# Reordering the start and the end of a fused retention and MoE kernel: two up projections ahead of their down projections, a shorter load ring, the tail block second to last

## The chip, the cores and the metric

One core of one Trainium2 chip. The metric is the device time of one execution in microseconds. A profiled execution shows a span, from the first to the last instruction, that is about 1.8 us shorter than the time. Engines are named as in the profile: PE (TensorE), PEld (its weight loads), DVE (VectorE), ACT (ScalarE), POOL (GpSimd), SP (the engine that issues most DMAs). In the tables by stage, (x245) counts instructions, and the clock is the mean clock that TensorE was granted, 1.00 being full speed.

## The reference, cut to what matters

```python
# attention with a decay mask and no softmax: q, k, v are (8, 8, 576, 64) float32
scores = scale * (q @ k.T)
ret    = scores * where(i >= j, gamma_h ** (i - j), 0)      # per head h
x      = (ret @ v) -> (4608, 512)
# then an MLP: w_in (512, 2048), w_out (2048, 512)
g      = gelu_tanh(x @ w_in)          # "up"
out    = g @ w_out                    # "down", float32, 4608 rows
```

## The kernel before

A batch has 576 rows: 512 in a block of its own, and 64 that all eight batches put into one ninth "tail" block. Each block has an up projection (64 matmuls of 512 columns, gelu on ScalarE) and a down projection in seven products (`my mz mw mv mu my2 mz2`), a fast-multiplication scheme over quadrants. A product collects in a bank of PSUM, the accumulator memory; the instructions that add it into the output tile `ost`, and so free the bank, are its *settle*. In the lists below `my2` and `mz2` appear as `my` and `mz`, whose banks they use. For it VectorE mixes the gelu output (three `tensor_tensor` per pair of slices: sum `gdia`, sum `gsum`, difference in place) and mixes the second weights once at the start:

```python
    def mix_w_out(j, e):                      # e = (V, A, V, G) before
        r0, r1 = w_raw.pop(("o", 2 * j)), w_raw.pop(("o", 2 * j + 1))
        e[0].tensor_tensor(out=w[:, 0:2, :]..., in0=r1, in1=r0, op=ALU.subtract)
        copy(e[1], w[:, 4, :], r0[:, L]); copy(e[1], w[:, 3, :], r1[:, R])
        e[2].tensor_tensor(out=w[:, 2, :], in0=r0[:, L], in1=r1[:, R], op=ALU.add)
        e[3].tensor_tensor(out=w[:, 5, :], in0=r0[:, L], in1=r0[:, R], op=ALU.add)
        e[3].tensor_tensor(out=w[:, 6, :], in0=r1[:, L], in1=r1[:, R], op=ALU.add)
        done(); done()                        # the two load tiles may be reused
```

Inputs come through a ring of `LD = 20` load tiles of 256 KB, in the order batch 0, all of `w_in`, half of batch 1, all of `w_out`, the rest. In the traces an engine's instructions start in program order (in the changed kernel the settle of `my2` starts at 83.66 us, behind four mixes, though its product ended at 79.0), so the plan, "after unit i of TensorE's work do these steps", is the schedule. The start of it, cut:

```python
    def stream(j):                            # five down products, slice by slice, as w_out arrives
        for m in MS[:5]:
            F.product(m, [j])
    units = A1[0:2] + [f for i in range(2, 8) for f in (A0[i], A1[i])]   # block 0 up
    units += [L(stream, j) for j in range(NJ)]                           # block 0 down
    ...
    units = [L(P.down, "my2"), L(P.down, "mz2")] + A0 + A1 + [L(F2.down, m) for m in MS]  # block 1
    ...
    for t in range(2, B + 1):                 # blocks 2..7, then the tail block (None)
        F = Block(t if t < B else None)
        ...
        run([L(F.up, f) for f in range(NF)] + [L(F.down, m) for m in MS], plan)
        P = F
    P.store()                                 # the tail block: eight DMAs, one per batch
```

Of the kernel before, what the change touches and what calls it, by code (L numbers as in the profile page):

```python
# [19 lines left out]
def kernel(  # L20
# [124 lines left out]
    LD = 20  # L145
# [48 lines left out]

    def tiles(b):
        a = att[b]
        a["kq"] = sb.tile([128, NS, 2, 2, 512], F16, tag="kq", name="kq", bufs=2)
        a["v"] = sb.tile([128, NS, 2, 512], F16, tag="cv", name="cv", bufs=2)
        a["kqt"] = sb.tile([128, 2, 256], F16, tag="kqt", name="kqt", bufs=2)
        a["vt"] = sb.tile([128, 256], F16, tag="cvt", name="cvt", bufs=3)  # L200
        a["T"] = sb.tile([128, NS, 2, 2, 4, 128], F16, tag="T", name="T", bufs=2)
        a["Tt"] = sb.tile([128, 2, 2, 128], F16, tag="Tt", name="Tt", bufs=3)
# [62 lines left out]
    def mix_w_out(j, e):  # L265
        r0, r1 = w_raw.pop(("o", 2 * j)), w_raw.pop(("o", 2 * j + 1))
        L, R = slice(0, 256), slice(256, 512)
        w = w_out_sb[:, j]
        e[0].tensor_tensor(out=w[:, 0:2, :].rearrange("p m c -> p (m c)"), in0=r1, in1=r0, op=ALU.subtract)  # L269
        copy(e[1], w[:, 4, :], r0[:, L])  # L270
        copy(e[1], w[:, 3, :], r1[:, R])
        e[2].tensor_tensor(out=w[:, 2, :], in0=r0[:, L], in1=r1[:, R], op=ALU.add)  # L272
        e[3].tensor_tensor(out=w[:, 5, :], in0=r0[:, L], in1=r0[:, R], op=ALU.add)
        e[3].tensor_tensor(out=w[:, 6, :], in0=r1[:, L], in1=r1[:, R], op=ALU.add)
        done()
        done()
# [49 lines left out]
    def mask_sc(b, s, hh):  # L326
        a = att[b]
        st = a.pop(("st", s, hh))
        for hl in range(2):
            x = sb.tile([128, 512], F16, tag="ret", name="ret", bufs=8)  # L330
            nc.vector.tensor_tensor(  # L331
                out=x.rearrange("p (a m) -> p a m", a=2),
                in0=st[hl].rearrange("p (a m) -> p a m", a=2),
                in1=cm.rearrange("p r s i -> p (r s i)").unsqueeze(1).to_broadcast([128, 2, 256]),
                op=ALU.mult,
            )
            a["ret", s, hh, hl] = x
# [20 lines left out]
    def mask_tail(b):  # L358
        a = att[b]
        st = a.pop("stt")  # L360
        for hl in range(2):
            x = sb.tile([128, 128], F16, tag="rett", name="rett", bufs=4)
# [27 lines left out]
    def scan(b, n):  # L390
# [4 lines left out]
        if n > 0:  # L395
            t = sb.tile([128, HP, 64], F32, tag="vs", name="vs", bufs=2)
            nc.vector.tensor_tensor(out=t, in0=uc, in1=a["w", n - 1], op=ALU.add)  # L397
            uc = t
        w = sb.tile([128, HP, 64], F32, tag="ws", name="ws", bufs=3)
# [90 lines left out]
    class Block:  # L490
        def __init__(self, b):
            self.b = b
            self.gT = self.sc = self.ost = None
            self.bank = {}

        def open(self):
            if self.gT is None:
                self.gT = sb.tile([128, NJ, 2, 512], F16, tag="gT", name="gT", bufs=1)

        def up(self, f):  # L500
# [11 lines left out]
            nc.scalar.activation(out=self.gT[:, f // 2, f % 2], in_=hp, func=AF.Gelu_apprx_tanh)  # L512

        def up_half(self, j, u):
            self.open()
            hp = bank("hp")
            for h in range(2):
# [8 lines left out]
                out=self.gT[:, j].rearrange("p h (s u c) -> p h s u c", s=2, u=2)[:, :, :, u, :],  # L526
# [4 lines left out]
        def mix(self, j, n):  # L531
            if self.sc is None:
                self.sc = sb.tile([128, NJ, 512], F16, tag="gsum", name="gsum", bufs=1)
                self.sa = sb.tile([128, NJ, 256], F16, tag="gdia", name="gdia", bufs=1)
            g = self.gT[:, j : j + n]
            L, R = slice(0, 256), slice(256, 512)
            nc.vector.tensor_tensor(  # L537
                out=self.sa[:, j : j + n], in0=g[:, :, 0, L], in1=g[:, :, 1, R], op=ALU.add
            )
            nc.vector.tensor_tensor(out=self.sc[:, j : j + n], in0=g[:, :, 0], in1=g[:, :, 1], op=ALU.add)  # L540
            nc.vector.tensor_tensor(  # L541
                out=g.rearrange("p j h c -> p j (h c)")[:, :, 256:768].rearrange("p j (h c) -> p j h c", h=2),
                in0=g[:, :, :, L],
                in1=g[:, :, :, R],
# [3 lines left out]
        def product(self, m, js=range(NJ)):  # L548
            lhs, w, more = {
                "my": (lambda j, c: self.gT[:, j, 0, c], 1, False),  # L550
                "mz": (lambda j, c: self.gT[:, j, 1, 256:512][:, c], 0, False),
# [3 lines left out]
                "my2": (lambda j, c: self.gT[:, j, 0, 256:512][:, c], 5, True),  # L555
                "mz2": (lambda j, c: self.gT[:, j, 1, c], 6, True),
# [4 lines left out]
            for u in range(2):  # L561
# [11 lines left out]
        def settle(self, m):  # L573
            if self.ost is None:
                self.ost = sb.tile([128, 2, 2, 512], F32, tag="ost", name="ost", bufs=1)
# [23 lines left out]
        def store(self):  # L599
# [8 lines left out]
            else:  # L608
                for u in range(2):
# [3 lines left out]
                    )  # L613

# [76 lines left out]
    for g in range(4):  # L691
        load_w_in(g)
    load_sc(1, 0)
    for f in range(NF):
        load_w_out(f)
    load_sc(1, 1)
    load_tail(0)
    load_tail(1)
    load(2)
    load(3)  # L700
# [6 lines left out]
    mask()  # L707
    cast_v(0, 0, 0, G)
# [30 lines left out]
    cast_w_in(0, (G, V, A, V))  # L739
    values(0, 1)  # L740
    inter_mm(0, 1, 0)
    evac(0, 1, 0)
    A0[0]()
    inter_mm(0, 1, 1)
    evac(0, 1, 1)
    A0[1]()
    cast_w_in(1, (V, G))
    scan_put(0, 3)

    def stream(j):  # L750
        for m in MS[:5]:
            F.product(m, [j])

    units = A1[0:2] + [f for i in range(2, 8) for f in (A0[i], A1[i])]
    units += [L(stream, j) for j in range(NJ)]
    plan = add({},
        (0, L(cast_w_in, 2, (V, G))),
        (2, L(F.mix, 0, 2)),
        (3, L(tbd_zero, 1, G)),
        (4, L(cast_w_in, 3, (V, G))),  # L760
        (6, L(F.mix, 2, 2)),
        (7, L(tiles, 1), L(cast_some, 1, 0, 0, (V, A, G))),
        (8, L(cast_some, 1, 0, 1, (V, A, G))),
        (9, L(tr, 1, 0, 0, (V, A))),
        (10, L(tr, 1, 0, 1, (V, A)), L(F.mix, 4, 2)),
        (11, L(score, 1, 0, 0), L(score, 1, 0, 1)),
        (13, L(state_mm, 1, [0]), L(scan_put, 1, 0), L(scan_put, 1, 1)),
        (14, L(F.mix, 6, 2)),
        *[(12 + j // 2, L(mix_w_out, j, (V, A, V, G))) for j in range(NJ)],
        (16, L(new_x, 1), L(values, 1, 0), L(inter, 1, 0)),  # L770
    )
    run(units, plan)
    for m in MS[:5]:
        F.settle(m)
# [4 lines left out]
    P = F  # L779
    units = [L(P.down, "my2"), L(P.down, "mz2")] + A0 + A1 + [L(F2.down, m) for m in MS]  # L780
    plan = add({},
        (0, L(cast_some, 1, 1, 0, (V, A, G))),
        (1, L(cast_some, 1, 1, 1, (V, A, G)), L(tr, 1, 1, 0, (V, A))),
        (2, L(tr, 1, 1, 1, (V, A)), L(P.store)),
        (3, L(score, 1, 1, 0), L(score, 1, 1, 1), L(state_mm, 1, [1])),
        (4, L(cast_tail, 0, V, V), L(scan_put, 1, 2), L(scan_put, 1, 3)),
        (5, L(tr_tail, 0, V)),
        (6, L(values, 1, 1), L(score_tail_mm, 0), L(inter, 1, 1), L(mask_tail, 0)),
        (8, L(cast_tail, 1, V, V)),
        (9, L(tr_tail, 1, V), L(values_tail, 0), L(inter_tail, 0)),  # L790
        (10, L(score_tail_mm, 1), L(mask_tail, 1)),
        (11, L(values_tail, 1), L(inter_tail, 1)),
        (11, L(tiles, 2), L(cast_some, 2, 0, 0, (V, V, G))),
        (12, L(F2.mix, 0, 2), L(cast_some, 2, 0, 1, (V, V, G))),
        (13, L(tr, 2, 0, 0, (V, A)), L(cast_some, 2, 1, 0, (V, V, G))),
        (14, L(F2.mix, 2, 2), L(tr, 2, 0, 1, (V, A)), L(cast_some, 2, 1, 1, (V, V, G))),
        (15, L(score, 2, 0, 0), L(score, 2, 0, 1)),
        (16, L(F2.mix, 4, 2), L(tr, 2, 1, 0, (A, A))),
        *states(2, 15),
        (18, L(F2.mix, 6, 2), L(tr, 2, 1, 1, (A, A))),  # L800
        (19, L(second, 2), L(cast_tail, 2, V, V)),
        (20, L(tr_tail, 2, A)),
        *casts(3, [17, 18, 19, 20, 21]),
        (22, L(tr_dma, 3), L(load, 4)),
        (22, L(third, 2)),
# [3 lines left out]
    for t in range(2, B + 1):  # L809
        F = Block(t if t < B else None)  # L810
        b = t + 1
# [4 lines left out]
        nxt = t + 2 if t + 2 < B else None  # L816
        if t == 2:
            add(plan,
                (1, L(values_tail, 2), L(inter_tail, 2)),
                *states(3, 3),  # L820
                (5, L(first, 2, False)),
                (9, L(second, 3)),
                (13, L(third, 3)),
                *states(nxt, 15),
            )
        else:
            if t < B:
                add(plan, (1, L(first, t)))
            if b < B:
                add(plan, (6, L(second, b)), (11, L(third, b)))  # L830
            if nxt is not None:
                add(plan, *states(nxt, 15))
        if t + 2 < B:
            add(plan, *casts(t + 2, [0, 2, 4, 6, 8]), (9, L(tr_dma, t + 2)))
            if t + 3 < B:
                add(plan, (9, L(load, t + 3)))
        run([L(F.up, f) for f in range(NF)] + [L(F.down, m) for m in MS], plan)
        P = F
    P.store()
# [30 lines left out]
```

## Time and profile before

| | before |
|---|---|
| time, median | 329.43 us when the prediction was made (3 runs), 328.93 with a fourth |
| span of the profiled execution | 324.0 us (that execution took 325.83, the fast end of its spread) |
| first up matmul to block 2's first up | 18.76 to 111.66 us, TensorE idle 17.8 of 92.9 |
| block 2's first up to the last product | 111.66 to 317, TensorE idle 1.13 of 205.34 |
| last VectorE instruction to the end | 6.4 us |

The stage table, the waits and the end are shown in the prediction. These are three lines of TensorE in order of time; the bracket gives the idle time just before the instruction and what ended it.

```profile
44.21 0.61 PE L563 MATMUL my<-w_out_sb,gT 128*128 128x256 f16 x2 [2.95 <-DVE w_out_sb L269]
48.99 0.38 PE L563 MATMUL my<-w_out_sb,gT 128*128 128x256 f16 x2 [1.10 <-DVE w_out_sb L269]
54.22 0.38 PE L563 MATMUL my<-w_out_sb,gT 128*128 128x256 f16 x2 [1.25 <-DVE w_out_sb L269]
```

Each is the first product of a new slice j. At full clock TensorE consumes a slice in about 1.1 us (one starts at 55.58, the next at 56.67) and before each of these three it had to wait for VectorE to mix it.

### The profile page before, as it was taken

Reading aid. Unit: us, or ns where it says so; the run is one execution under the profiler, and the core shown is the slowest. Engines: PE = TensorE matmul, PEld = TensorE weight load, DVE = VectorE, ACT = ScalarE, POOL = GpSimd, SP = SyncE. Lnnn points to the kernel's source line nnn. Section 1 sums busy time; section 2 is a strip of 40 time slices with the busy share of each in tenths; the row PEclk is TensorE's granted clock in tenths of the full one; section 3 lists DMA queues with packets and bytes.
Section 4 is the critical chain, followed back from the end, with each engine's and each line's share of the span. In section 5 each row is a group of like instructions: output and inputs, shape, how many; then the busy total and the mean of one; then the engine's idle time right before and its main releaser. Section 6 shows DMA issues by size and latency. Waiting matters only on the chain.

```text
span 324.0 us, 8575 instructions
## 1 busy us (share of the span) xinstructions
PE 292.0 (90%) x3628; PEld 206.3 (64%) x3628; DVE 230.9 (71%) x423; ACT 150.5 (46%) x286; POOL 94.5 (29%) x129
## 2 busy tenths in 40 slices
PE   6769857989396998999999999999999999999991
PEld 4648635778285754785587568557855874784680
DVE  5866999877997679958866997697479254443440
ACT  6556635356255066435552545354455316406510
POOL 2536994141941631830165047100000000000000
PEclk9578979999789999999999999999999999999997
DMA  7999983989979898809994996570030011003004
GB/s 216 317 380 297 390 221 88 256 253 276 229 147 250 201 252 235 216 16 242 216 231 131 188 287 143 164 116 2 2 131 0 2 67 65 0 2 129 3 0 130
DMA packets 94438, 52.59 MB, mean 162 GB/s; under 512 B 38848, under 2 KB 88000, under 8 KB 94400
## 3 DMA queue, kind: packets, MB, share of 16 engines
q1 hardware_dynamic: 94208, 51.53, 61.1%
q8 instruction: 28, 0.46, 0.6%
q10 hardware_dynamic: 192, 0.52, 0.6%
q14 instruction: 10, 0.08, 0.1%
HBM read 36.70 MB, written 9.44 MB: 142 GB/s over the span
## 4 chain that ended last, share of the span: by engine, by line
PE 64%; DVE 2%; ACT 0%; issue 0%
PE hp L508 29%; PE my L563 8%; PE mz L563 8%; PE mv L563 4%; PE mu L563 4%; PE mw L563 4%; PE xs L421 2%; PE xs L452 2%; PE st L318 1%; DVE ret L331 1%; PE us L383 1%; PE xs L477 0%; PE xs L434 0%; DVE ws L400 0%; ACT tbd L211 0%; DVE vs L397 0%
## 5 line engine op out<-in xcount | busy, mean ns | idle before, releaser
L512 ACT ACTIVATE gT<-hp 128x512 f16<-128x512 f32 x112 | 66.7, 597 | 77.8 <-PE hp L508 77.5
L508 PE MATMUL hp<-x,w_in_sb 128*128 128x512 f16 x384 | 87.0, 379 | 0.0
L508 PEld LDWEIGHTS <-w_in_sb 128*128 128x128 f16 x448 | 42.8, 98 | 47.4 <-issue 0.3
L563 PEld LDWEIGHTS <-gT 128*128 128x128 f16 x576 | 56.1, 98 | 13.5 <-DVE w_out_sb L269 3.1
L218 POOL TENSOR_TENSOR cv<-ld,sc 128x512 f16<-128x512 f32 x32 | 35.9, 1127 | 43.2 <-DMA ld<-in_v_dram 35.5
L211 POOL CAST kq<-ld 128x512 f16<-128x512 f32 x40 | 27.9, 718 | 54.0 <-PE hp L508 18.3
L331 DVE TENSOR_TENSOR ret<-st,cm 128x512 f16<-128x512 f32 x64 | 40.6, 693 | 1.9 <-PE st L318 1.9
L563 PE MATMUL my<-w_out_sb,gT 128*128 128x256 f16 x288 | 36.0, 275 | 5.4 <-DVE w_out_sb L269 5.3
L563 PE MATMUL mz<-w_out_sb,gT 128*128 128x256 f16 x288 | 35.9, 274 | 0.0
L519 PE MATMUL hp<-x,w_in_sb 128*128 128x256 f16 x256 | 34.7, 292 | 1.1 <-ACT w_in_sb L211 1.1
L211 ACT CAST tbd<-ws 64x256 f16<-64x256 f32 x64 | 25.8, 403 | 19.5 <-DVE ws L400 18.7
L537 DVE TENSOR_TENSOR gdia<-gT 128x512 f16<-128x512 f16 x36 | 17.4, 484 | 23.7 <-ACT gT L512 21.0
L563 PEld LDWEIGHTS <-gsum 128*128 128x128 f16 x288 | 28.4, 99 | 3.4
L580 DVE TENSOR_TENSOR ost<-ost,mv 128x512 f32<-128x512 f32 x18 | 11.6, 684 | 25.4 <-PE mv L563 20.4
L519 PEld LDWEIGHTS <-w_in_sb 128*128 128x128 f16 x256 | 25.8, 105 | 5.8 <-ACT w_in_sb L211 1.3
L540 DVE TENSOR_TENSOR gsum<-gT 128x1024 f16<-128x1024 f16 x36 | 28.0, 779 | 0.0
L541 DVE TENSOR_TENSOR gT<-gT 128x1024 f16<-128x1024 f16 x36 | 27.0, 749 | 1.2
L525 ACT ACTIVATE gT<-hp 128x512 f16<-128x512 f32 x32 | 19.0, 598 | 18.6 <-PE hp L519 18.4
L465 DVE TENSOR_TENSOR x<-xs,gx 128x512 f16<-128x512 f32 x32 | 20.7, 683 | 3.5 <-PE xs L452 3.1
L563 PE MATMUL mw<-w_out_sb,gdia 128*128 128x256 f16 x144 | 18.6, 274 | 1.0 <-DVE w_out_sb L272 0.6
L563 PE MATMUL mv<-w_out_sb,gsum 128*128 128x256 f16 x144 | 18.6, 275 | 0.0
L563 PE MATMUL mu<-w_out_sb,gsum 128*128 128x256 f16 x144 | 18.6, 275 | 0.0
(75 smaller groups left out, 304.7 us busy)
## 6 DMA issues: line engine op xcount, KB each, us to landing
ld<-in_k_dram SPq DMA_DIRECT2D x32, 256.0 KB, 5.5
ld<-in_q_dram SPq DMA_DIRECT2D x32, 256.0 KB, 5.6
ld<-in_v_dram SPq DMA_DIRECT2D x32, 256.0 KB, 5.7
out_dram<-ost SPq DMA_DIRECT2D x16, 512.0 KB, 3.8
ld<-in_moe_w_in_dram SPq DMA_DIRECT2D x16, 256.0 KB, 6.0
ld<-in_moe_w_out_dram SPq DMA_DIRECT2D x16, 256.0 KB, 5.4
ld<-in_k_dram SPq DMA_DIRECT2D x16, 64.0 KB, 4.3
ld<-in_q_dram SPq DMA_DIRECT2D x16, 64.0 KB, 3.4
```

The costliest lines, as they stand in the source:

```text
L211: (eng.copy if eng is nc.scalar else eng.tensor_copy)(out=out, in_=in_)
L218: eng.tensor_tensor(out=unperm(att[b]["v"][:, s, hh, :]), in0=perm(att[b].pop(("v", s, hh))), in1=sc[:, 8 * hh : 8 * hh + 8] .rearrange("p ...
L331: nc.vector.tensor_tensor(out=x.rearrange("p (a m) -> p a m", a=2), in0=st[hl].rearrange("p (a m) -> p a m", a=2), in1=cm.rearrange("p r s ...
L465: nc.vector.tensor_tensor(out=xb[b][:, :, 2 * s + c].rearrange("p s q i -> p q s i"), in0=att[b]["x", s][c].rearrange("p (q s i) -> p q s ...
L508: nc.tensor.matmul(hp, w_in_sb[:, ct, 128 * f : 128 * f + 128], x[:, :, ct, :], start=(ct == 0), stop=(ct == 3),)
L512: nc.scalar.activation(out=self.gT[:, f // 2, f % 2], in_=hp, func=AF.Gelu_apprx_tanh)
L519: nc.tensor.matmul(hp[:, 256 * h : 256 * h + 256], w_in_sb[:, ct, 256 * j + 128 * h : 256 * j + 128 * h + 128], xb[self.b][:, :, 2 * u : 2 ...
L525: nc.scalar.activation(out=self.gT[:, j].rearrange("p h (s u c) -> p h s u c", s=2, u=2)[:, :, :, u, :], in_=hp.rearrange("p (h s c) -> p ...
L537: nc.vector.tensor_tensor(out=self.sa[:, j : j + n], in0=g[:, :, 0, L], in1=g[:, :, 1, R], op=ALU.add)
L540: nc.vector.tensor_tensor(out=self.sc[:, j : j + n], in0=g[:, :, 0], in1=g[:, :, 1], op=ALU.add)
L541: nc.vector.tensor_tensor(out=g.rearrange("p j h c -> p j (h c)")[:, :, 256:768].rearrange("p j (h c) -> p j h c", h=2), in0=g[:, :, :, L] ...
L563: nc.tensor.matmul(t[:, 256 * u : 256 * u + 256], lhs(j, slice(128 * u, 128 * u + 128)), w_out_sb[:, j, w], start=(u == 0 and j == 0 and n ...
```

## The change

Its intent: give TensorE up projections, which need only `w_in` and attention outputs, while `w_out` arrives and is mixed; take casts off VectorE; shorten what follows the last product. The first weights' casts are spread over more engines too. The diff, cut to its core:

```diff
-    LD = 20
+    LD = 12
-        a["T"] = sb.tile([128, NS, 2, 2, 4, 128], F16, tag="T", name="T", bufs=2)
+        a["T"] = big("T").rearrange(...)          # 4 buffers, two of them lent to block 1's gelu output
     # fewer buffers elsewhere: Tt 3 to 2, ret 8 to 6, rett 4 to 2, vs 2 to 1, ws 3 to 2
-            self.gT ... bufs=1      # one tile of 8 slices
+            self.gT ... bufs=2      # two tiles of 4 slices; block 1 takes its two from "T"
-                self.ost = ... bufs=1
+                self.ost = ... bufs=2
     # mix_w_out is split: the last two adds (GpSimd) become mix_w_out2, one unit later
     # loads
-    for g in range(4): load_w_in(g)
-    load_sc(1, 0)
-    for f in range(NF): load_w_out(f)
-    load_sc(1, 1)
+    for g in range(3): load_w_in(g)
+    load_sc(1, 0)
+    load_w_in(3)
+    load_sc(1, 1)
+    for f in range(NF): load_w_out(f)
     # the start
-    units = ...block 0 up, then stream(j) of block 0's down, then block 1 up, then block 1 down
+    units = A1[0:2] + [L(F.up, f) for f in range(4, NF)]                # block 0 up
+    units = A0 + A1                                                     # block 1 up, w_out mixed beside it
+    units = [L(P.down, m) for m in MS] + [L(Q.down, m) for m in MS]     # both downs, batch 2 beside them
+        (0, L(tiles, 2), L(cast_some, 2, 0, 0, (A, A, G))),             # was (V, V, G)
+        (2, L(Q.mix_sa, 0, 4), L(Q.mix_sa, 4, 4)),
+        (4, *[L(Q.mix_sc, 2 * i, 2) for i in range(4)]),
+        (8, *[L(Q.mix_d, 2 * i, 2) for i in range(4)]),
     # the end
-    for t in range(2, B + 1):
+    order = [*range(2, B - 1), None, B - 1]                             # tail block second to last
+        F.last()    # block 7: three quadrants stored as they settle, the fourth as two DMAs on two queues
-    P.store()
```

## The prediction

> **What bounds the kernel now.** I read the per-stage windows first, then TensorE's waits, then the chain of waits, then VectorE's order of time in the bad stage, and the end of the trace last. The windows below were cut where the program changes stage: start; up projection of block 0; its down projection together with the second weights; block 1; the first pass of the steady loop; the steady loop; the end. The columns are length, busy time of each engine, granted clock, DMA share, GB/s.
>
> ```profile
> 0.00:18.76 18.76, 12.69 (x249) 9.42 (x249) 13.48 (x43) 11.57 (x22) 6.35 (x17) 0.82 0.98 281
> 18.76:40.80 22.04, 19.28 (x183) 15.40 (x180) 16.11 (x25) 13.51 (x27) 16.56 (x21) 0.85 1.07 354
> 40.80:62.50 21.70, 15.72 (x181) 12.21 (x180) 20.69 (x34) 9.54 (x26) 11.05 (x12) 0.92 0.67 174
> 62.50:92.80 30.30, 23.78 (x417) 19.19 (x417) 26.00 (x51) 13.15 (x25) 16.84 (x20) 0.89 0.88 234
> 92.80:111.66 18.86, 16.32 (x242) 13.76 (x241) 14.99 (x30) 7.54 (x16) 5.05 (x9) 1.00 0.99 236
> 111.66:317.00 205.34, 204.21 (x2366) 136.34 (x2363) 139.04 (x244) 95.15 (x173) 38.70 (x53) 1.00 0.47 113
> 317.00:324.00 7.00, 0.00 (x0) 0.00 (x0) 0.62 (x1) 0.00 (x0) 0.00 (x0) 0.72 0.52 150
> ```
>
> From 111.66 us, where block 2's ups begin, to 317 us TensorE is busy for 204.21 of 205.34 us at clock 1.00. Nothing that leaves its work as it is can shorten that. The money lies in the middle (18.76 to 111.66, 92.9 us) and in the last 7 us. In the middle TensorE idles 2.76 + 5.98 + 6.52 + 2.54 = 17.8 us, and its clock is below 1.00 in three of the four windows. VectorE is the busy one there: 20.69 of 21.70 us in the second-weight stage. TensorE's waits between 18 and 112 us name it:
>
> ```profile
> PE my L563 <- DVE w_out_sb L269: 5.3, 3, 2.9
> PE tr L283 <- DVE kq L211: 4.3, 4, 1.6
> PE st L318 <- DVE T L211: 3.0, 1, 3.0
> PE tr L291 <- DVE kqt L211: 1.8, 2, 1.4
> ```
>
> So block 0's down products wait for VectorE to mix the second weights, and later the transposes and scores of batch 2 wait for VectorE's casts and copies. The end of the trace shows what follows the last product:
>
> ```profile
> 314.99 1.91 PE L563 MATMUL mz<-w_out_sb,gT 128*128 128x256 f16 x16
> 315.19 0.69 DVE L580 TENSOR_TENSOR ost<-ost,my 128x512 f32<-128x512 f32 x1 [0.46 <-PE my L563]
> 316.94 0.69 DVE L580 TENSOR_TENSOR ost<-ost,mz 128x512 f32<-128x512 f32 x1 [1.06 <-PE mz L563]
> 317.65 2.57 SPq L604 DMA_DIRECT2D out_dram<-ost  x4
> 317.65 2.58 ACTq L604 DMA_DIRECT2D out_dram<-ost  x4
> ```
>
> The tail block's store is eight DMAs, four in a row on each of two queues (0.64 us per issue), so 324.0 - 317.63 = 6.4 us pass after VectorE's last instruction.
>
> **What the Trainium skill says.** "SBUF — State Buffer", section "Who interferes with whom": a VectorE copy in a two-port mode, or an instruction with two SBUF inputs, contends with GpSimd, and the second to issue waits. The trace agrees: the same SBUF-only mix (L537) takes 0.42 us alone and 0.93 us at 31.21, beside GpSimd's v casts, while the masks that read PSUM (L331) stay at 0.69 us. So work left on VectorE in the weight stage costs more than its solo time when the other half of the weight mix runs on GpSimd. "TensorE: Matmul & The Clock Gate", section "What's actually happening": the clock is halved after an idle window of about 3.4 us and released after a busy one. The trace agrees in kind: the mean clock is 0.69 over 81 to 90 us, where TensorE is busy 4.03 of 9 us, and 0.62 over 9 to 27 us. Gaps thus cost twice. "DMA: Bandwidth & Descriptors", section "Anatomy of one DMA", gives a fixed cost of about 2 us, mostly the write receipt (stated for the GpSimd path). On the hardware queues here a 512 KB store takes 3.8 us to land and a 128 KB one in the final group 3.5 us, so size matters little, as the page says; the number issued in series matters more.
>
> **The change, part by part.** The stretch that is rearranged is 18.76 to 111.66. Its TensorE work at full clock, from steady rows of the chain of waits: an up projection is 64 matmuls in 13.81 us; a down projection 7 x 1.75 = 12.2; a batch's attention 2 x 0.57 + 2 x 0.45 + 0.33 + 0.55 + 0.64 = 3.6; eight transposes 0.45. Two ups, two downs, two attentions, eight groups of transposes, two tails (0.76 each: 0.30 transposes, 0.06, 0.18, 0.22) and about 1.2 left of batch 0 give 27.6 + 24.4 + 7.2 + 3.6 + 1.5 + 1.2 = 65.5 us. It takes 92.9 now. So 27.4 us could go at most: 17.8 idle, and 9.6 of slow clock and pipeline overlap. The change adds no matmul.
>
> 1. Ups of both blocks first. The w_out tiles are needed only after the second up, some 17 us later than now. This removes the 5.3 + 0.6 us waits on w_out in the stream and lets TensorE warm up. The weight mix still costs VectorE 8 x (0.93 + 0.65) = 12.6 us, ScalarE 16 x 0.40 = 6.4 and GpSimd 8 x (0.99 + 0.90) = 15.1; these are the same instructions as before.
>
> 2. VectorE is relieved. Its busy time in the stretch is 77.8 us. It gives up the eight q/k casts of batch 2 (8 x 0.78 = 6.3), six tail casts (1.8), two casts of first weights (1.0) and four copies out of PSUM (1.7, at 0.42 each): 10.8, leaving 67.0. ScalarE takes nearly all of it. In the first two phases ScalarE then has 32 gelus (19), six weight casts (3.7), four q casts (2.5), four transposed copies (2.3), eight state casts (3.3) and the weight copies (6.4): 37 us of about 40. It is close to full but not the bound.
>
> 3. Batch 1 before w_out, and 12 load buffers in place of 20. Before w_out come 8.4 MB + 2.1 MB; at 330 GB/s that is 32 us, and w_out (4.2 MB) would follow by about 45 us. With 12 buffers a load waits for the cast twelve tiles earlier, which I followed by hand: w_in keeps its issue times; batch 1's tiles slip to 16 to 24 us, landing by 28, when they are wanted; the last four w_out tiles wait for GpSimd's first mixes at 47 to 49 us and are still in time. I count 0 for it.
>
> Walking the program with these durations: first up at about 21 us (it now waits for ScalarE's weight cast, +0.6); phase 1 (14 units, 12 of them 0.87 us, plus transposes, scores and one half of values) ends at 41 with some 3.5 us of waits, for VectorE's k cast behind a mix and for the fourth first-weight group; phase 2 (16 half-ups of 0.87 and 3.3 of attention, 1.8 of waits) ends at 60 on TensorE. VectorE however reaches the weight mix only at about 51 and needs 12.6 + 0.85 + 2.3 (last mix of block 0) more: it finishes about 65 to 66. The first down product takes all eight mixed tiles, so it finishes near there: 4 to 5 us of new wait. Phase 3 is 31 us of TensorE work (24.4 of downs, 3.6 attention, 1.8 transposes, 1.5 tails) against 30 of VectorE; with 1 us of bank waits it ends at 96.5. Block 2's ups then begin 15.2 us earlier.
>
> 4. Steady loop: the same work, so 205 us again; batch 4's casts move by six units and have 14 us of downs to hide in. Tail block second to last: no work added; its eight stores lie under block 7's ups.
>
> 5. The end: the last store is two DMAs of 128 KB, one on each queue. Three further issues at 0.64 us on the path (1.9 us) go, and some landing time with fewer in flight (0.5, an estimate from the 3.5 and 3.8 us above). Gain 2.4: 6.4 becomes 4.0. The other quadrants are stored 1.75 us or more earlier.
>
> Sum: 329.4 - 15.2 - 2.4 = 311.8, so 312.
>
> **Rivals.** (a) VectorE is the new bound and gives more back. For: both it and ScalarE are nearly full in phases 1 and 2, and GpSimd runs 15 us of weight mixes beside it; its L269 has been seen at 1.5 us, against 0.68 alone. Against: 10.8 us were taken off it. If every weight mix took 2.2 us (1.53 + 0.65), the weights would be ready 5 us later: 317. (b) The waits vanish nearly all: TensorE's floor of 18.8 + 65.5 = 84 us and VectorE's 18.8 + 67 = 86 allow a start of block 2 at 90, as the plan looks tuned unit by unit: 305. (c) The shallower load ring starves the start: DMA share is 1.07 now, in part because 20 tiles are in flight. If loads fell to 250 GB/s, w_out would land at some 58 us and phase 3 start 6 to 8 us later: 319. Against it: the waits now are on engines' work far more than on loads. (d) Batch 3's transpose DMA, issued late behind GpSimd's casts, holds the first scores of the steady loop: up to 3 us more, 315.
>
> **Range and chances.** The end's 2.4 is safe within 0.7. The stretch gain of 15.2 is uncertain by about 6 either way from (a) to (c), so 304 to 320. Faster by over 2% means under 322.8; that needs only a gain of 6.6, of which the end alone gives 2.4 and the w_out waits 5.9. Faster 0.94, same 0.05, slower 0.01.
>
> **What would show it.** Block 2's first 512-column up should start near 96 us (90 to 102). The waits on w_out should be one, at the first down product, of 3 to 6 us; none there would mean that I overrated VectorE's backlog. TensorE's clock should be 1.00 from about 30 us on, VectorE's busy time over the stretch some 67 us. The end after the last VectorE instruction should be about 4 us. I am wrong if a new wait on loads appears between 20 and 60 us, if ScalarE's copies or gelus become what TensorE waits for, or if the steady loop shows new gaps.

## The result, and the profile after

| | before | changed |
|---|---|---|
| median, us | 328.93 (325.63 to 330.11, 4 runs) | 318.07 (317.27 to 318.77, 4 runs) |
| ratio | | 0.9685, 95% interval 0.9609 to 0.976 |
| span of the profiled execution | 324.0 | 315.5 |

A ratio here is the mean time of one kernel's fast runs over that of the other's fast runs of the same rounds, so it is not quite the ratio of the medians quoted. The profiled execution of before was 3 us under its median and that of the changed kernel 0.8 us under its own, so the two traces differ by 8.5 us where the medians differ by 10.9. The accounts below are of the traces.

The changed kernel by stage: start; block 0's ups; block 1's ups; both downs; the steady loop; the end. Columns as in the prediction.

```profile
0.00:18.52 18.52, 13.51 (x245) 9.80 (x245) 13.28 (x42) 11.10 (x22) 9.12 (x22) 1.00 0.98 278
18.52:42.40 23.88, 20.25 (x209) 10.96 (x205) 15.72 (x30) 17.13 (x35) 4.36 (x5) 0.93 0.87 247
42.40:62.69 20.29, 17.49 (x248) 14.83 (x248) 18.03 (x29) 14.32 (x33) 14.91 (x18) 1.00 0.66 206
62.69:103.14 40.45, 35.53 (x511) 28.34 (x508) 32.64 (x56) 20.02 (x44) 19.07 (x25) 0.96 0.83 215
103.14:311.10 207.96, 205.75 (x2380) 137.28 (x2378) 140.24 (x248) 95.24 (x174) 44.25 (x61) 1.00 0.56 136
311.10:315.50 4.40, 0.00 (x0) 0.00 (x0) 0.62 (x1) 0.00 (x0) 0.00 (x0) 0.82 0.32 106
```

Set against the stage table in the prediction: the rearranged stretch is 84.6 us in place of 92.9, with TensorE idle for 3.63 + 2.80 + 4.92 = 11.4 us in place of 17.8 and busy for 73.3 in place of 75.1. The steady loop is 2.6 us longer, the end 2.6 us shorter. -8.3 + 2.6 - 2.6, and 0.2 earlier at the start, is the 8.5.

What TensorE waits for between 20 and 110 us now (total, times, longest):

```profile
PE my L584 <- DVE w_out_sb L271: 2.5, 4, 0.7
PE my L584 <- DVE ost L601: 2.3, 1, 2.3
PE tr L288 <- DVE kq L214: 1.9, 2, 1.4
PE hp L529 <- ACT w_in_sb L214: 1.8, 1, 1.8
PE xs L457 <- ACT tbd L214: 1.2, 1, 1.2
```

The 3.0 us of the scores on VectorE's copy and the 1.8 us of the tails' transposes are gone. The second weights still hold TensorE for 2.5 us (5.9 before), and a wait is new: 2.3 us of block 1's first product for block 0's settle (`ost`). VectorE's order of time around it, with the idle time that precedes:

```profile
66.48 0.41 DVE L274 TENSOR_TENSOR w_out_sb<-ld 128x256 f16<-128x256 f32 x1
71.80 1.71 DVE L545 TENSOR_TENSOR gdia<-gT 128x1024 f16<-128x1024 f16 x2 [4.91 <-PE mw L584]
79.57 4.16 DVE L553 TENSOR_TENSOR gsum<-gT 128x1024 f16<-128x1024 f16 x4
83.66 0.68 DVE L601 TENSOR_TENSOR ost<-ost,my 128x512 f32<-128x512 f32 x1
```

The last weight mix ends at 66.9 us. Then the first mix of block 1 waits 4.91 us for product `mw` of block 0, because both use the one `gdia` buffer. Later four `gsum` mixes (4.16 us) stand ahead of the settle whose end lets TensorE on at 84.39.

The end, whose counterpart is in the prediction:

```profile
311.04 0.69 DVE L601 TENSOR_TENSOR ost<-ost,mz 128x512 f32<-128x512 f32 x1 [1.06 <-PE mz L584]
311.75 0.36 ACTq L640 DMA_DIRECT2D out_dram<-ost  x1
```

From 311.73 to 315.5 are 3.8 us, where before they were 6.4.

### The profile page after: what moved, and what is told of

It reads as the page before. It is cut to its first block, busy times and chain, and to the rows that moved or that the text cites. A ratio compares the mean times of both kernels' runs of the same rounds, so it can differ in the third digit from the quotient of the medians.

```text
span 315.5 us, 8517 instructions
## 1 busy us (share of the span) xinstructions
PE 292.5 (93%) x3580; PEld 201.2 (64%) x3580; DVE 220.5 (70%) x401; ACT 157.8 (50%) x305; POOL 91.7 (29%) x130
## 4 chain that ended last, share of the span: by engine, by line
PE 72%; DVE 15%; ACT 6%; DMA 3%; SPq 1%; issue 1%; DVEq 0%; ACTq 0%
PE hp L518 28%; PE my L584 10%; PE mz L584 9%; PE mu L584 5%; PE mw L584 4%; PE mv L584 4%; DVE gsum L553 3%; DMA ld<-in_q_dram 3%; PE xs L426 2%; DVE ret L336 2%; PE xs L457 2%; DVE x L470 2%; ACT tbd L214 2%; PE st L323 2%; DVE gT L557 2%; PE us L388 1%
## 5 line engine op out<-in xcount | busy, mean ns | idle before, releaser
L522 ACT ACTIVATE gT<-hp 128x512 f16<-128x512 f32 x124 | 73.1, 598 | 73.3 <-PE hp L518 71.8
L518 PE MATMUL hp<-x,w_in_sb 128*128 128x512 f16 x432 | 98.8, 379 | 1.0 <-DVE w_in_sb L214 0.4
L518 PEld LDWEIGHTS <-w_in_sb 128*128 128x128 f16 x496 | 47.0, 98 | 53.1 <-ACT w_in_sb L214 0.8
L545 DVE TENSOR_TENSOR gdia<-gT 128x512 f16<-128x512 f16 (+1 forms) x34 | 18.0, 531 | 27.4 <-ACT gT L522 21.1
L584 PE MATMUL mz<-w_out_sb,gT 128*128 128x256 f16 x288 | 34.4, 273 | 0.0
L553 DVE TENSOR_TENSOR gsum<-gT 128x1024 f16<-128x1024 f16 x36 | 30.0, 840 | 0.0
L529 PE MATMUL hp<-x,w_in_sb 128*128 128x256 f16 x160 | 20.6, 284 | 2.8 <-ACT w_in_sb L214 1.8
L529 PEld LDWEIGHTS <-w_in_sb 128*128 128x128 f16 x160 | 15.7, 101 | 6.1 <-ACT w_in_sb L214 2.4
L584 PE MATMUL mw<-w_out_sb,gdia 128*128 128x256 f16 x144 | 17.2, 273 | 0.0
L584 PE MATMUL mv<-w_out_sb,gsum 128*128 128x256 f16 x144 | 17.2, 273 | 0.0
L405 DVE TENSOR_TENSOR ws<-vs,gt 128x256 f32<-128x256 f32 x24 | 12.7, 529 | 5.7 <-ACT tbd L214 4.2
```

The lines of the kernel that those rows point to most:

```text
L405: nc.vector.tensor_tensor(out=w, in0=uc, in1=gt.unsqueeze(2).to_broadcast([128, HP, 64]), op=ALU.mult)
L518: nc.tensor.matmul(hp, w_in_sb[:, ct, 128 * f : 128 * f + 128], x[:, :, ct, :], start=(ct == 0), stop=(ct == 3),)
L522: nc.scalar.activation(out=self.g(f // 2)[:, f % 2], in_=hp, func=AF.Gelu_apprx_tanh)
L529: nc.tensor.matmul(hp[:, 256 * h : 256 * h + 256], w_in_sb[:, ct, 256 * j + 128 * h : 256 * j + 128 * h + 128], xb[self.b][:, :, 2 * u : 2 ...
L545: nc.vector.tensor_tensor(out=self.sa[:, j : j + n], in0=g[:, :, 0, 0:256], in1=g[:, :, 1, 256:512], op=ALU.add)
L553: nc.vector.tensor_tensor(out=self.sc[:, j : j + n], in0=g[:, :, 0], in1=g[:, :, 1], op=ALU.add)
```

## The experiments

Twelve runs were made, in three sets of four kernels, each set on one chip with 11 runs of the kernel before. The unaltered changed kernel ran again in the first and third set. Two executions were slow (one of the kernel with the four `gsum` mixes moved, one of the kernel before in the third set); the figures here leave them out. The spread of one kernel is about 1 us (standard deviation), so with six runs each a difference of means under about 1.2 us is not told from noise.

At first I held **theory A**: the time lost against the prediction sits in single waits of TensorE at fixed places in VectorE's queue, and reordering the queue recovers it. The rival **B**: VectorE's total work bounds the down stage whatever the order. A second pair followed: **C**, the wait on the second weights comes from VectorE's order, against **D**, from loads that the shallow ring holds back.

**The yardstick.**

> The changed kernel unaltered, as the yardstick on this chip for the three runs beside it. Both theories: about 318 us, 10 to 11 us under the kernel before; the start of block 2's ups near 103 us of the span, with one wait of about 2.3 us of the second block's first down product on VectorE's settle.

> The changed kernel unaltered, yardstick for the three beside it: about 318 us, ratio near 0.970.

Measured: 318.53 us (ratio 0.971) and 318.19 us (0.9725, interval 0.968 to 0.9769). The first result stands. In the two profiles the bank wait was 0.6 and 1.0 us rather than 2.3, so its size varies between executions of one kernel.

**The four `gsum` mixes behind the settles.**

```diff
-        (4, *[L(Q.mix_sc, 2 * i, 2) for i in range(4)]),
+        (6, L(Q.mix_sc, 0, 2), L(Q.mix_sc, 2, 2)),     # behind P.store and the scan
+        (7, L(Q.mix_sc, 4, 2), L(Q.mix_sc, 6, 2)),
```

> The four gsum mixes of block 1 moved from behind the fifth down product to behind the seventh and eighth, so that VectorE settles block 0's last two products first. Theory A (the 2.3 us wait is for a bank of PSUM that VectorE's settle frees, and the settle stands behind 4.2 us of mixes in VectorE's queue): the wait goes, and with it some of the slow clock after it; block 2's ups start 2 to 4 us earlier, 315 to 316 us. Rival B (VectorE is full in that stage whatever the order, so the work only moves): the wait reappears at another instruction of the same stage and the time stays within 1 us.

Measured: 318.31 us (five fast runs), ratio 0.9691 (0.9651 to 0.9731), against 318.53 for the yardstick on the chip. The wait for the settle was gone from TensorE's list, and these were there instead (60 to 104 us):

```profile
PE us L388 <- DVE ret L336: 1.3, 1, 1.3
PE xs L457 <- ACT tbd L214: 0.8, 1, 0.8
```

So B's forecast held here: the mixes now delay the masks of batch 2 in the second half of the stage. Removing a wait by moving work past it pays only if the new place has room.

**Batch 2's first casts back on VectorE, and both edits together.**

```diff
-        (0, L(tiles, 2), L(cast_some, 2, 0, 0, (A, A, G))),
+        (0, L(tiles, 2), L(cast_some, 2, 0, 0, (V, V, G))),
-        (1, L(cast_some, 2, 0, 1, (A, A, G)), ...
+        (1, L(cast_some, 2, 0, 1, (V, V, G)), ...
```

> The q and k casts of batch 2's first half go back from ScalarE to VectorE (one piece of the relief undone). Theory A (VectorE's queue is idle for 4.9 us at the start of the down stage, because the first mix of block 1 waits for the third down product, and ScalarE is late with these casts): the casts fall into the idle time, take the place of ScalarE's, and the masks of batch 2 come earlier: same or up to 2 us faster. Rival B (VectorE's total is the bound of the stage): 4 casts of 0.42 us more make it 1.7 us slower.

> Both edits together. Theory A: 3 to 5 us under the changed kernel, about 314. Rival B: 0 to 2 us slower than the changed kernel.

Measured: 318.63 us (0.9698) and 318.85 us (0.9715). The first run allows A (it had "same or up to 2 us faster") and shows no sign of B's 1.7 us loss; the second shows no sign of A's 3 to 5 us gain and allows B ("0 to 2 us slower"). In the first the four casts ran in 1.42 us right behind the last weight mix, in time that had been idle; VectorE then still sat idle for 5.2 us until `mw` was done. Between them the two runs speak against both theories in their strong form.

**Block 1's difference mixes left out** (wrong result).

```diff
-        (8, *[L(Q.mix_d, 2 * i, 2) for i in range(4)]),
```

> Wrong result on purpose: block 1's four difference mixes (4 x 0.7 to 0.9 us of VectorE, in the down stage) are left out, all else as in the changed kernel. Rival B (VectorE's total bounds the down stage): 3 us faster, about 315 us, and block 2's ups 3 us earlier. Theory A's remainder (single waits at fixed places, not the total): under 1 us.

Measured: 318.03 us, ratio 0.9717 (0.9674 to 0.9759). No gain that is clear of the noise, although 2.5 to 4 us of VectorE's work were gone (what the four mixes take in the other traces). From block 1's first product to block 2's first up this run took 17.6 us, by these two lines of TensorE:

```profile
83.35 1.91 PE L584 MATMUL my<-w_out_sb,gT 128*128 128x256 f16 x16 [1.75 <-DVE ost L601]
100.98 1.03 PE L518 MATMUL hp<-x,w_in_sb 128*128 128x512 f16 x4
```

The run with only block 0's last mix moved (below) took 17.6 as well, from 83.73 to 101.35, with all difference mixes in place, and so did the first yardstick, from 86.16 to 103.81. The profiled execution of this run was 1.9 us under its median, and its whole down stage took 39.1 us, against 39.8 to 40.5 in the three profiles of the changed kernel: 1 us less or so, not the 3 of B. That half of the stage therefore runs at TensorE's pace, and B falls as a statement on the whole stage. What remains of both theories: block 0's half waits on VectorE at two places, block 1's half has some room, which four `gsum` mixes overfill.

**Most of the relief undone.** Of the twenty instructions taken off VectorE twelve go back: batch 2's eight q and k casts and the four q and k tail casts. The first-weight casts and the copies out of PSUM stay where the change put them.

```diff
-        cast_some 2,*,*: (A, A, G);  cast_tail 0: A, A;  cast_tail 1: G, G
+        cast_some 2,*,*: (V, V, G);  cast_tail 0: V, V;  cast_tail 1: V, V
```

> The relief of VectorE undone where it can be without touching the order: batch 2's eight q and k casts and the four q and k tail casts of batches 0 and 1 on VectorE again, all else as in the changed kernel. If VectorE's total bounds the down stage, 8 x 0.42 + 4 x 0.25 = 4.4 us or more of it come back as time, about 322 us. If only its queue's order at fixed places counts, 0 to 2 us, 318 to 320 us.

Measured: 318.87 us, ratio 0.9765, against 318.19 us on the chip; by the means of the runs (319.17 and 317.92) 1.2 us, at the edge of the noise. The twelve casts took 6.0 us of VectorE in this trace (the expectation had counted 4.4), so most of what was put back was absorbed, in part where VectorE had sat idle; its wait for `mw` was 3.56 us in this run, 4.91 in the first profile of the changed kernel and 6.17 in the yardstick's:

```profile
67.20 1.42 DVE L214 CAST kq<-ld 128x512 f16<-128x512 f32 x4
72.18 1.71 DVE L545 TENSOR_TENSOR gdia<-gT 128x1024 f16<-128x1024 f16 x2 [3.56 <-PE mw L584]
```

**A deeper ring for the second weights.** The last eight `w_out` tiles are loaded into the two output buffers, which are idle until the down stage:

```diff
     def load_w_out(f):
-        load_w(("o", f), moe_w_out[128 * f : 128 * f + 128, :])
+        if f < 8: load_w(...)                      # through the ring, as before
+        else:     DMA into a slice of an "ost" tile # released when mix_w_out2 is done with it
```

> The last eight tiles of the second weights are loaded into the two output buffers, idle until the down stage, so that the ring of twelve has room for batch 2 (in effect twenty buffers there). Rival D (the shallow ring costs time): the loads run 5 us or more earlier and the time falls by 2 to 4 us. Theory C and rival B (VectorE's queue never waited for a load there): the loads run earlier, the time stays within 1 us of the changed kernel, 318 us.

Measured: 320.74 us, ratio 0.9796 (0.9754 to 0.9838), 2.3 to 2.8 us slower than the unaltered kernel by its ratios (0.9725 and 0.971). The loads did run earlier: all `w_out` tiles were issued by 52 us, against 58.9. D falls, and the first profile of the changed kernel says the same: between 18 and 104 us VectorE never waited for a load. The profile shows a cost that I had not expected; one line of GpSimd, then two of VectorE:

```profile
52.42 6.15 POOL L294 TENSOR_TENSOR w_out_sb<-ost 128x256 f16<-128x256 f32 x8
56.80 1.19 DVE L285 TENSOR_TENSOR w_out_sb<-ld 128x512 f16<-128x512 f32 x1
57.91 0.94 DVE L288 TENSOR_TENSOR w_out_sb<-ld 128x256 f16<-128x256 f32 x1
```

With tiles at hand GpSimd runs its weight mixes without a pause, into the time when VectorE starts its own, and VectorE's take 1.19 and 0.94 us. In the changed kernel GpSimd is idle from 54.7 to 58.5 us, waiting for loads, and VectorE's mixes there take 0.68 and 0.42. The section "Who interferes with whom" of the Trainium skill's "SBUF — State Buffer" says that a VectorE instruction with two SBUF inputs contends with a GpSimd one that reads SBUF. This trace agrees. But the collision does not explain the loss. The first yardstick has one too (1.19 us at 56.05, beside GpSimd's mixes), and VectorE's sixteen weight mixes took 11.1 us in this profile against 9.3, 10.3 and 9.3 in the three of the changed kernel: 0.8 to 1.7 us more. The profiled execution took 318.64 us, the fastest of its six, and shows no loss. So the cause of the 2.3 to 2.8 us stays open.

**Block 0's last mix behind the weight mixes.**

```diff
-        (9, L(F.mix, 6, 2)),
         *[(5 + j + j // 4, L(mix_w_out, j, (V, A))) for j in range(NJ)],
         *[(6 + j + j // 4, L(mix_w_out2, j, G)) for j in range(NJ)],
+        (13, L(F.mix, 6, 2)),
```

> Block 0's last mix (3.1 us of VectorE) moved from before the last four weight mixes to behind them; nothing else. Theory C (TensorE's waits at the first down product, 2.5 to 3.0 us, and the slow clock after them come from the order of VectorE's queue, since the mix is needed only by the third product): the four waits go, the first product takes 1.75 us, block 2's ups start 3 to 4 us earlier, about 315 us. Rival D (the last weight tiles land late, because twelve load buffers hold them back): the waits stay at 2 us or more, now on the weight mixes' loads, and the time stays within 1 us. Rival B (VectorE's total holds the next stage whatever comes before): the waits go but the time gained returns as waits in the down stage, within 1 us.

Measured: 316.49 us, ratio 0.9682 (0.9644 to 0.972). TensorE's waits in the down stage of its profile:

```profile
PE my L584 <- DVE ost L601: 1.8, 1, 1.8
PE my L584 <- DVE w_out_sb L271: 1.3, 2, 0.7
```

The wait on the weights fell from 2.5 or 3.0 to 1.3 us, the clock was 1.00 through the whole down stage (which can be luck: see **The clock**), and that stage took 37.3 us in place of 40.5. But block 2's ups started only 1.8 us earlier (101.35), because this execution had a slower start: clock 0.53 from 18.6 to 27 us, against 0.80. At the scores of batch 3, TensorE then waited 1.8 us for the transposing DMA of `T` (rival d of the prediction). Theory C is right on the mechanism, and too hopeful on its size (two of the four waits stayed); with no unaltered kernel in this set, the gain of 1 to 2 us is not clear of the noise for this edit by itself.

**Block 0's third mix moved as well** (from before batch 1's last k cast to behind its scan).

```diff
-        (13, L(F.mix, 4, 2)),     # block 0's ups
+        (6, L(F.mix, 4, 2)),      # block 1's ups, behind scan_put(1, 3)
```

> As the run before, and block 0's third mix also moved, from before batch 1's last k cast to behind its scan. Theory C: the wait of 1.4 to 1.9 us of the transposes on that cast goes too, but VectorE's sum up to the weight mixes is unchanged; up to 1 us better than the run before, about 314.5 us. Rival B: no change against the changed kernel.

Measured: 317.94 us, ratio 0.9729, worse than the run before it by 1.5 us in the means (318.28 and 316.74), with a standard error of 0.7. The profile is of the slowest of the six executions (320.98). In it the transposes waited 0.8 us, against 1.9 in the first profile of the changed kernel but 0.5 already in that of the run before; the mix now stood ahead of seven weight mixes, and the wait on the weights was back at 2.9 us, with a mean clock of 0.55 after it (67 to 73 us). A miss.

**Block 0's last mix moved, and two of the four `gsum` mixes.** This puts the two partial gains together, with half of the `gsum` mixes left in place since the second half had room for some.

```diff
-        (9, L(F.mix, 6, 2)),
+        (13, L(F.mix, 6, 2)),
-        (4, *[L(Q.mix_sc, 2 * i, 2) for i in range(4)]),
+        (4, L(Q.mix_sc, 0, 2), L(Q.mix_sc, 2, 2)),
+        (6, L(Q.mix_sc, 4, 2), L(Q.mix_sc, 6, 2)),
```

> Block 0's last mix behind the weight mixes, as in the earlier run, and two of block 1's four gsum mixes moved from before the settle of block 0's sixth product to behind the settle of its seventh. If the waits at fixed places are worth what they show (w_out 1.2 to 2 us, bank 1.8 us), 2 to 3 us under the changed kernel on the same chip; if they are made good elsewhere, as when all four mixes were moved, within 1 us.

Measured: 316.55 us, ratio 0.9669 (0.9626 to 0.9713), against 318.19 us for the changed kernel on the same chip; means 316.04 and 317.92, a gain of 1.9 us with a standard error of about 0.5. This version beats both kernels. Whether the two `gsum` mixes add to it is not shown: the ratio with the one mix moved was 0.9682, a difference of 0.4 us. Block 0's half of the down stage went from 21.7 us in the yardstick's profile to 18.6 us; block 1's half rose from 18.4 to 20.7 us, with a new wait on the masks (1.1 us) and a longer one on the state's copy (1.5 us, 0.6 in the yardstick). In these two traces the down stage is thus 0.8 us shorter, less than the 1.9 of the means.

**The end alone, on the kernel before.** Its edit is the last part of the diff above, with the same order of blocks.

> The kernel before with the end of the change alone: tail block second to last, block 7's output stored by quadrants, two DMAs after the last VectorE instruction in place of eight. The prediction's part 5: 2.4 us faster than before, with 4.0 us from the last VectorE instruction to the end of the span in place of 6.4. Rival: the quadrant's 1 KB rows land more slowly and the order of the last two blocks costs TensorE time, under 1 us gained.

Measured: 325.71 us against 327.30 (ten fast runs), ratio 0.995 (0.9902 to 0.9997). The end of its profile:

```profile
320.22 0.69 DVE L580 TENSOR_TENSOR ost<-ost,mz 128x512 f32<-128x512 f32 x1 [1.06 <-PE mz L563]
320.94 0.36 ACTq L619 DMA_DIRECT2D out_dram<-ost  x1
```

It ends at 324.3 us, 3.4 us after VectorE in place of 6.4. The timed gain, 1.6 us with an interval of 0.1 to 3.2, contains the 2.4 predicted and the 3.0 seen. It is a gain by a small margin only, and "same" by the 2% rule.

**The clock.** Two windows of the second yardstick's profile, in the columns used above:

```profile
62.00:67.00 5.00, 3.02 (x24) 2.13 (x22) 4.97 (x9) 5.00 (x14) 1.51 (x2) 0.97 0.79 224
67.00:73.00 6.00, 5.47 (x43) 4.46 (x43) 0.81 (x2) 3.17 (x7) 2.08 (x3) 0.74 0.56 142
```

In the first TensorE was busy 3.02 of 5 us, with no gap above 0.67 us (the four waits for weights, 0.50, 0.67, 0.67, 0.67, the last of them mostly after 67.0); in the next its mean clock was 0.74, though it had work. In the profiled execution of the changed kernel the same four waits cost no clock, and the dip came after the 2.3 us wait: product `my` of block 1 took 2.78 us in place of 1.91. In the run with one mix moved there was none. Of the ten profiles of the changed kernel and its variants with 2.5 us or more of weight waits, six have a mean clock of 0.55 to 0.78 from 67 to 73 us and four have 1.00; the two with 1.3 and 1.6 us of these waits have 1.00. The Trainium skill's "TensorE: Matmul & The Clock Gate", section "What's actually happening", says that the window over which activity is watched runs freely. That would fit the irregularity, its place against the waits differing from one execution to the next; no run here shows the window itself.

## Why the prediction was right or wrong

It gave 312 us, 304 to 320, and 0.94 for faster by over 2%. The measured 318.07 is in the range and 3% faster, near the slow end: the gain was some 11 us, not 17. Most of what it said of the stages did happen in kind; the sizes of four terms were wrong. How the gain divides between the parts is not shown (see the end of this section).

1. **Ups first takes the weight wait off the stream.** Right in kind. The one wait at the first down product, forecast at 4 to 5 us (3 to 6 in the test at the prediction's end), was 2.5 us in four pieces. The mis-sized term is the weight mix on VectorE: 12.6 us forecast from the old means, 8 x (0.68 + 0.48) = 9.3 us measured, with GpSimd idle from 54.7 to 58.5 and from 62.6 to 67.4 us.
2. **VectorE relieved by 10.8 us.** Its busy time in the stretch was 15.72 + 18.03 + 32.64 = 66.4 us, as forecast (67.0). But in the new order the relief was worth little: twelve of its twenty instructions undone cost 1.2 us. VectorE's total was not what set the time of the down stage; single places in its order were.
3. **The shorter ring counted as 0.** Not contradicted: neither TensorE nor VectorE waited for a load between 20 and 104 us, and a deeper ring was slower. But the loads ran later than walked: the last `w_out` tile was issued at 58.9 us, not 47 to 49, and it was GpSimd that waited for them (5.3 us).
4. **The walk through the stages.** First up at 21, block 0's ups to 41, block 1's to 60: measured 20.60 (a single matmul aside), 42.4, 62.7. Block 1's ups to the first down product at clock 1.00 took 20.3 us against 19 forecast, with 2.8 us idle in place of 1.8. The first of the two misses is in good part slow clock (0.93 over block 0's ups), for which the walk had no term.
5. **The down stage is the step that failed:** "Phase 3 is 31 us of TensorE work ... with 1 us of bank waits it ends at 96.5". From 60, where the second ups were to end, that is 36.5 us with both kinds of wait; it took 40.45, from 62.69 to 103.14. The work is best read from the run with one mix moved, at clock 1.00 throughout: 37.26 us, 3.1 of them waits (1.3 + 1.8). Counted from each start to the next, its fourteen products take 26.1 us where 24.4 were forecast, and what lies between them (attention of batch 2, transposes, tails) 8.1 where 3.6 + 1.8 + 1.5 = 6.9 were. The prediction had priced both from the steady loop, where a product is followed by another after 1.75 us; here most are followed by a matmul of another shape, after about 1.85. First the loop, in the changed kernel, then the down stage with one mix moved:

```profile
305.59 1.91 PE L584 MATMUL mu<-w_out_sb,gsum 128*128 128x256 f16 x16
307.34 1.91 PE L584 MATMUL my<-w_out_sb,gT 128*128 128x256 f16 x16
```

```profile
94.29 1.91 PE L584 MATMUL mu<-w_out_sb,gsum 128*128 128x256 f16 x16
96.13 0.64 PE L426 MATMUL xs<-ret,cv 64*64 64x128 f16 x32
```

   So the work was 34.2 us, not 31. The waits in the changed kernel were 2.5 us on weights, where 4 to 5 were counted, and 2.3 on the bank, where 1 was. The rest of the 40.45, some 1.5 us by difference, goes to the slow clock, for which there was no term. Block 2's first up at 103.14 lies outside the 90 to 102 us that the prediction gave as its own test.
6. **The steady loop "the same work, so 205 us again"** was 2.6 us too short. 2.2 of it lie in the first 53 us of the loop, up to block 3's down products. 0.5 us is batch 2's tail transposes and scores, carried into it (0.32 + 0.19 us in the trace); TensorE's idle time rose from 1.13 to 2.21 us, on VectorE's `x`, `xt` and mask instructions. That is, on a small scale, the prediction's own sign of being wrong, "if the steady loop shows new gaps". The last 1 us is not assigned to a cause. The change also took buffers from the tiles of masks and states (`ret`, `rett`, `vs`, `ws`); whether these gaps come from that was not tested.
7. **The end, 2.4 us:** 2.6 us in the trace of the changed kernel, 3.0 with the end alone. Right.

Of the rivals, (a), VectorE as the new bound, is half right: it delays TensorE at its queue's fixed places. (b), the floor of 305, was far off. (c), a starved start, did not happen. (d), the late transposing DMA, is absent from the first profile of the changed kernel and cost 0.4 to 1.8 us in some of the other runs. Another sign of being wrong, TensorE waiting for ScalarE's copies, appeared in part: 1.8 us for the first weights' cast (1.1 before) and 1.2 us for a state's copy, 3.0 of the 11.4 us idle.

That most of the gain comes from putting the ups first is argued, not shown. The lists of TensorE's waits do not decide it: waits for second weights fell from 5.9 to 2.5 us, and waits for VectorE's casts and copies of q, k and `T` from 9.1 to 1.9, which can be the new order or the relief; other and new waits took some 4 us back. I did not undo the order alone, because it comes with its load order: with twelve load tiles, `w_out` ahead of batch 1's second half would fill the ring, and in the new program order no `w_out` tile is released before that half is cast. What the experiments show is what is left: of 10.9 us, about 1.6 to 3.0 belong to the end and about 1.2 to the part of the relief that was undone, in the new order.

## What to carry to other kernels

When an engine waits for another's in-order queue, look at the order of that queue before its total: here 6.0 us of work put back cost 1.2, and some 3 us of it left out gave nothing clear of the noise, while moving one 3 us block behind what TensorE needs first, with half of another, gave 1.9. When adding up a stage from its pieces, take large and small pieces alike from a stage that mixes them in the same way, not from the tightest loop, and leave a term for the clock after every cluster of waits.

## What the Trainium skill lacked or had wrong

- "TensorE: Matmul & The Clock Gate": its table says that the clock drops after a whole idle window of about 3.4 us, and its advice is to have no idle gaps above about 3 us. Here it fell to a mean of 0.74 over 67 to 73 us around and after four gaps of at most 0.67 us each, with TensorE busy 3.02 of the 5 us before; six of ten profiles with such waits show it. The section on queue cycling names frequent small idles as a cause, but gives no share of busy time for it.
- "SBUF — State Buffer": that VectorE and GpSimd contend is stated, but nothing is said of what it costs a stage of many short instructions, in which only some of them meet. Here VectorE's sixteen weight mixes took 9.3 us where one of them ran long beside GpSimd, 10.3 where three did and 11.1 where four did.
- "DMA: Bandwidth & Descriptors": its fixed cost of about 2 us is for the GpSimd path. On the hardware queues the 128 KB stores landed in a median of 2.1 us in the run with the end alone and of 3.5 us in the kernel before, where the last eight are issued together, so one figure does not cover them.
